# A gated linear attention with an MLP behind it: the odd angles of 64 partitions travel in the carry tile, and the kernel gets another order of work

## The chip, the cores and the metric

The kernel runs on one core of one Trainium2 chip. The metric is the device time of one execution in microseconds (us), the median of three runs. All times below are microseconds unless marked ns. The engines are named as in the profile: PE (matrix products), PEld (loading of their weights), DVE (vector), ACT (scalar and table functions), POOL (general purpose), SP (which only issues DMAs here).

## The reference, cut to what matters

```python
# q, k, v, a_re, a_im: (4 batches, 8 heads, 768 steps, 48)
mag = sqrt(a_re**2 + a_im**2);  scale = minimum(mag, 0.999) / (mag + 1e-6)
ar, ai = a_re * scale, a_im * scale
for t in range(S):                                   # a complex state, 48 x 48 per head
    new_re = ar[t] * S_re - ai[t] * S_im
    new_im = ar[t] * S_im + ai[t] * S_re
    S_re, S_im = new_re + outer(k[t], v[t]), new_im
    y[t] = q[t] @ S_re
x  = y with the heads side by side                   # (4, 768, 384)
xn = (x - mean(x)) / sqrt(var(x) + 1e-6) * g_ln
out = x + maximum(xn @ w_ch1, 0) @ w_ch2             # 384 -> 1536 -> 384
```

The recurrence is computed in chunks of 128 steps. The logarithm of the gate's size and its angle are summed over the steps, which gives decays and phases; q and k are multiplied by them, and what is left is a masked product of q and k, times v, plus the state of the chunk before.

## The kernel before, in words

There are 4 batches of 6 chunks. Two chunks make a **pair**, so there are 12 pairs, P = 0 to 11; chunks are numbered n = 2P and 2P + 1. The first pair of a batch is P = 0, 3, 6, 9. Pair 0 is worked in two halves of four heads (parts), all others in one piece.

For a pair, a partition holds **two neighbouring steps**: partition p has step 2p (j = 0, "even") and 2p + 1 (j = 1, "odd") of the pair's 256. In this layout ACT takes a logarithm (`ln`), an inverse (`iv`), `u` and the arctangent (`th`), and DVE or POOL the products `r` and `r2` and the log-size `l`. Running sums over the steps are products on PE with triangles of ones (`u_e` for sizes, `u_th` for angles in turns), which leave chunk c = 0 and c = 1 in two PSUM banks with one step to a partition. `dec` is the sum of sizes, from which ACT makes the decays `e` and `en`; `ph` is the sum of angles. Chunk 0 needs the odd angles of partitions 0 to 63 alone (the triangle `u_th[:, 0, 1]` is zero below them), chunk 1 needs all.

The **carry**: a phase runs on from pair to pair of a batch. After `ph` of a pair, `car.P` writes rows 96 to 127 of the next pair's tile `car` (fp16, 128 x 384, two in turn) with the last phases; row 64 holds a constant window (`car0`, the tile is filled with it once). `pick` is a weight that is 1 in rows 64 and 127 and 0 elsewhere, so a product with it adds window and carry; `pick_f`, for a batch's first pair, has row 64 alone. A pair's `ph` before is six products of 384 columns: two of angles for each chunk, and one of the carry for each.

From the phases ACT makes sine and cosine (`sin`, `cos`, with `abs` or `qt` between), `ke`, `qe` multiply k and q by the decays, and `ks`, `qs` by sine and cosine. `ksT`, `qsT` are their transposes: on PE through PSUM (`kT`, `qT`, then a copy), or as a DMA transpose that SP issues. `am` is the product of both, `atm` its masking on DVE, `gm` and `G` the state, `y` the output, `x` its copy, `xtr` and `xT` its transpose, `mm1`, `relu` and `mm2` the MLP, `ot` the last sum, and `st` the store. `wp` and `wc` fold the norm into the first weight at the start (weights come by `wl`).

**What sets the order.** One table, `PLAN`, names every step, its engine (P, A, V, G for POOL, S for a DMA issued by SP) and its PSUM bank; each engine runs its steps in this order, and semaphores are placed from what a step reads and writes. `@name` behind a step lets it wait for another on purpose (turns between POOL and DVE). `warm` steps are products of no use (256 columns of `u_e`) that keep PE busy while the first inputs come. A step on the S list waits in line behind those before it; `k`, `q`, `vf`, `are`, `aim` are loads.

```python
for op in steps:
    ...
    op.emit()
```

Of the kernel before, what the change touches and what calls it, by code (L numbers as in the profile page):

```python
# [51 lines left out]
warm.69:P0 warm.70:P0 warm.71:P0 warm.72:P0 warm.73:P0 warm.74:P0 warm.75:P0 dps.0:P5 mask:G are.3.0:S r2.2.0:V
e.1.0:A2 dps.1:P7 ke.0.1.0:V u.2.0:A tab.trig.1:A pad.qs.1:G th.0.1:A vf.0.1:S ke.0.0.0:V th.0.0:A th.1.0:A warm.76:P0
warm.77:P0 warm.78:P0 warm.79:P0 warm.80:P0 warm.81:P0 warm.82:P0 warm.83:P0 warm.84:P0 warm.85:P0 warm.86:P0
warm.87:P0 warm.88:P0 warm.89:P0 warm.90:P0 ph.0.1:P1 qe.0.0.0:V decc.0:V5 qe.0.1.0:V decc.1:V7 l.2.0:V sin.0.1:A1
vf.0.0:S ph.0.0:P3 lc.2.0:V car.0.1:A1 car.0.0:V3 ks.0.1.1:V qs.0.1.1:V warm.91:P0 warm.92:P0 wp.1:P4 wc.1.2:V4
qt.0.1:P1 k.1.1:S wl.0:G th.2.0:A ph.1.0:P6 wc.1.1:V4 wc.1.0:V4 sin.0.0:A3 ke.1.0.0:G@qs.0.1.1 qs.0.0.1:V aim.3.0:S
cos.0.1:A1 qt.0.0:P3 qe.1.0.1:G sin.1.0:A6 cos.0.0:A3 qs.0.1.0:V tab.log.2:A ks.0.0.0:V warm.93:P0 warm.94:P0
warm.95:P0 warm.96:P0 warm.97:P0 warm.98:P0 warm.99:P0 warm.100:P0 warm.101:P0 dec.2.0:P4 ks.0.1.0:V qs.0.0.0:V
q.2.0:S warm.102:P0 warm.103:P0 warm.104:P0 warm.105:P0 warm.106:P0 warm.107:P0 wp.0:P1 en.2.0:A4 ks.0.0.1:V  # L60
qe.1.0.0:G@qs.0.0.0 car.1.0:V6 wc.0.0:V1 kT.0:P2 e.2.0:A4 wc.0.2:V1 qT.0:P3 vf.1.0:S qt.1.0:P6 vf.1.1:S qsT.0:V3
qT.1:P5 ln.3.0:A qs.1.0.1:G warm.108:P0 warm.109:P0 warm.110:P0 warm.111:P0 kT.1:P3 are.4.0:S ksT.0:A2 q.2.1:S
wc.0.1:V1 qsT.1:V5 iv.3.0:A wl.2:G ksT.1:V3 warm.112:P1 am.0:P0 k.2.1:S aim.4.0:S k.2.0:S warm.113:P2 ph.2.0:P4
am.1:P2 tab.trig.3:A atm.0:V0 atm.1:V2 cos.1.0:A6 v.0:G ke.1.0.1:G warm.114:P0 warm.115:P0 gm.0:P7 y.0:P1 sin.2.0:A4
warm.116:P0 warm.117:P0 qt.2.0:P4 G.0:A7 x.0:A1 qs.1.0.0:V gm.1:P7 y.1:P2 cos.2.0:A4 r.3.0:G xtr.0:P6 x.1:A2
ks.1.0.0:V warm.118:P0 qT.3:P1 pad.qs.2:G qT.2:P4 v.1:G th.3.0:A ks.1.0.1:V xT.0:V6 r2.3.0:G@xT.0 xtr.1:P3 kT.3:P0
qsT.3:V1 wp.2:P6 wl.3:G@xT.0 ksT.3:V0 q.3.1:S qsT.2:A4 tab.log.4:A kT.2:P2 qe.2.0.1:G qe.2.0.0:G am.3:P4 xT.1:V3
G.1:V7 mm1.0.0.1:P0 mm1.0.0.0:P0 one:G@ke.0.1.0 ksT.2:A2 gm.2:P7 relu.0.0:A0 wc.2.0:V6 atm.3:V4 wc.2.2:V6 G.2:A7
mm1.0.1.1:P2 ln.4.0:A am.2:P4 mm1.0.1.0:P2 wc.2.1:V6 y.3:P6 relu.0.1:A2 ph.3.0:P0 iv.4.0:A atm.2:V4 x.3:V6 gm.3:P7
y.2:P6 qs.2.0.1:V x.2:A6 xtr.3:P2 mm1.0.2.1:P4 wl.4:G@atm.2 xtr.2:P3 car.3.0:V0 q.3.0:S r.4.0:G are.6.0:S mm1.0.2.0:P4  # L70
bn.1:V xT.3:V2 xT.2:V3 abs.3.0:A0 mm1.1.1.0:P2 u.3.0:A bn.3:V G.3:V7 relu.0.2:V4 mm1.1.1.1:P2 tab.trig.5:A relu.1.1:A2
mm1.1.2.1:P6 sin.3.0:A0 k.3.0:S bn.2:V mm1.1.2.0:P6 k.3.1:S mm1.1.0.0:P3 cos.3.0:A qs.2.0.0:V are.5.0:S mm1.1.0.1:P3
wl.5:G@qs.2.0.1 l.3.0:V th.4.0:A r2.4.0:V lc.3.0:V qT.5:P2 qT.4:P1 ke.2.0.1:G relu.1.2:V6 mm2.0.0:P5 mm2.0.1:P5
relu.1.0:A3 ke.2.0.0:G ks.2.0.0:G@r2.4.0 tab.log.6:A mm2.1.0:P3 u.4.0:A bn.0:V dec.3.0:P6 rstd.0:A mm2.1.1:P3 qsT.4:V1
# [137 lines left out]
def kernel(  # L212
# [12 lines left out]
    nc = tc.nc  # L225
# [617 lines left out]
```

## Time and profile before

| | us |
|---|---|
| three runs | 188.86, 189.84, 190.18; median 189.84 |
| the profiled execution, own time | 189.38 |
| its span on the core | 187.7 |
| busy PE / DVE / ACT / POOL | 175.9 / 159.0 / 156.0 / 95.7 |
| granted PE clock | 1.00 |

A page of the profile has the busy time of each engine, the span in 40 equal slices (digits are tenths busy), the DMA queues, the chain of work that ended last, and the costliest groups of instructions. PE's products are pipelined: the mean of one is its own length from start to end, while a run of them follows at a shorter distance, so the sum of a run is read from a run's length. Between the span and the execution's own time lie 1.68 us.

### The profile page before, as it was taken

Reading aid. Unit: us, or ns where it says so; the run is one execution under the profiler, and the core shown is the slowest. Engines: PE = TensorE matmul, PEld = TensorE weight load, DVE = VectorE, ACT = ScalarE, POOL = GpSimd, SP = SyncE. Lnnn points to the kernel's source line nnn. Section 1 sums busy time; section 2 is a strip of 40 time slices with the busy share of each in tenths; the row PEclk is TensorE's granted clock in tenths of the full one; section 3 lists DMA queues with packets and bytes.
Section 4 is the critical chain, followed back from the end, with each engine's and each line's share of the span. In section 5 each row is a group of like instructions: output and inputs, shape, how many; then the busy total and the mean of one; then the engine's idle time right before and its main releaser. Section 6 shows DMA issues by size and latency. Waiting matters only on the chain.

```text
span 187.7 us, 5141 instructions
## 1 busy us (share of the span) xinstructions
PE 175.9 (94%) x2040; PEld 138.6 (74%) x2040; DVE 159.0 (85%) x292; ACT 156.0 (83%) x223; POOL 95.7 (51%) x117
## 2 busy tenths in 40 slices
PE   5699999999999999999999999999999899797992
PEld 3488677888677897777877877877768577685772
DVE  0599999999989999889999899968999878676463
ACT  5699999999999999999999999988999869143220
POOL 8137387776614990696068570740621507521650
PEclk9999999999999999999999999999999999999999
DMA  5999999999999895899999999999989899996423
GB/s 136 284 243 178 235 237 213 209 191 227 228 235 265 188 263 131 147 219 213 187 244 206 181 245 218 179 227 171 213 188 197 190 210 155 234 121 167 136 98 126
DMA packets 131799, 37.23 MB, mean 198 GB/s; under 512 B 125888, under 2 KB 131776, under 8 KB 131776
## 3 DMA queue, kind: packets, MB, share of 16 engines
q1 hardware_dynamic: 128272, 33.76, 86.5%
q0 software_dynamic: 2784, 2.36, 8.5%
q10 hardware_dynamic: 720, 0.79, 1.2%
q8 instruction: 16, 0.26, 0.5%
q14 instruction: 7, 0.06, 0.1%
HBM read 28.31 MB, written 4.72 MB: 176 GB/s over the span
## 4 chain that ended last, share of the span: by engine, by line
PE 56%; DVE 19%; DMA 13%; issue 3%; SPq 3%; ACT 3%; POOL 1%; DVEq 0%; ACTq 0%; POOLq 0%
PE banks L773 20%; PE banks L741 14%; DMA aim<-in_a_im_dram 5%; DMA qsT<-qs 5%; PE banks L613 5%; PE banks L507 4%; PE banks L636 3%; DVE w1b L392 3%; DVE atm L293 3%; DMA ksT<-ks 2%; PE banks L481 2%; DVE r L293 2%; PE banks L686 2%; PE banks L707 2%; PE banks L689 2%
## 5 line engine op out<-in xcount | busy, mean ns | idle before, releaser
L773 PE MATMUL banks<-w2b,h 128*128 128x384 bf16 (+1 forms) x300 | 54.6, 319 | 0.0
L741 PE MATMUL banks<-xT,w1b 128*128 128x256 bf16 x432 | 51.2, 272 | 0.1
L741 PEld LDWEIGHTS <-w1b 128*128 128x128 bf16 x432 | 41.2, 98 | 6.5 <-DVE xT L290 0.8
L773 PEld LDWEIGHTS <-h 128*128 128x128 bf16 x300 | 26.8, 97 | 12.5
L293 DVE TENSOR_TENSOR atm<-banks,mask 128x1024 bf16<-128x1024 f32 x24 | 28.9, 1219 | 4.8 <-PE banks L636 4.5
L758 ACT ACTIVATE h<-banks 128x1024 bf16<-128x1024 f32 (+1 forms) x25 | 24.9, 1006 | 9.4 <-PE banks L741 9.2
L293 POOL TENSOR_TENSOR ke<-k,en 128x384 bf16<-128x384 f32 x17 | 15.8, 933 | 16.5 <-ACT en L485 4.7
L811 ACT ACT_TABLE_LOAD x18 | 23.1, 1283 | 1.1 <-PEq L827 0.8
L806 PE MATMUL banks<-u_e 128*128 128x256 f16 x119 | 16.7, 289 | 2.5 <-POOL u_e L322 2.2
L636 PE MATMUL banks<-qsT,ksT 128*128 128x128 bf16 x192 | 14.6, 219 | 2.9 <-DMA qsT<-qs 1.8
L760 DVE TENSOR_SCALAR h<-banks 128x1024 bf16<-128x1024 f32 (+1 forms) x12 | 14.0, 1175 | 3.7 <-PE banks L741 3.6
L293 POOL TENSOR_TENSOR qe<-q,e 128x384 bf16<-128x384 f32 x13 | 12.0, 929 | 9.3 <-DVE ks L293 5.3
L636 PEld LDWEIGHTS <-ksT 128*128 128x128 bf16 x192 | 12.2, 98 | 5.0 <-issue 2.3
L806 PEld LDWEIGHTS <-u_e 128*128 128x128 f16 x119 | 12.1, 104 | 4.6 <-POOL u_e L322 1.9
L293 POOL TENSOR_TENSOR r<-aim,are 128x768 f16<-128x768 f32 x6 | 10.9, 1813 | 6.1 <-ACT are L454 5.9
L786 POOL TENSOR_TENSOR ot<-ot,x 128x384 f32<-128x384 f32 x11 | 10.6, 974 | 6.3 <-DVE x L290 4.4
L288 ACT CAST x<-banks 128x384 bf16<-128x384 f32 x16 | 7.7, 483 | 7.2 <-PE banks L689 6.4
L470 DVE SCALAR_TENSOR_TENSOR l<-r,w 128x768 f16<-128x768 f16 (+1 forms) x13 | 12.9, 996 | 0.7 <-ACT r L466 0.6
L699 DVE BATCH_NORM_STATS2 stats<-x 128x6 f32<-128x384 bf16 x24 | 13.2, 550 | 0.3 <-ACT x L288 0.3
L293 POOL TENSOR_TENSOR qs<-qe,trig 128x768 bf16<-128x768 bf16 x6 | 10.3, 1725 | 5.9 <-DVE qe L293 3.5
L418 POOL TENSOR_SCALAR v<-vf 128x768 bf16<-128x768 f32 x8 | 7.0, 869 | 12.0 <-DMA vf<-in_v_dram 7.0
L686 PE MATMUL banks<-v,atm 128*128 128x48 bf16 x192 | 12.1, 183 | 0.2 <-DVE atm L293 0.2
(100 smaller groups left out, 385.0 us busy)
## 6 DMA issues: line engine op xcount, KB each, us to landing
k<-in_k_dram SPq DMA_DIRECT2D x24, 192.0 KB, 4.3
q<-in_q_dram SPq DMA_DIRECT2D x24, 192.0 KB, 4.5
vf<-in_v_dram SPq DMA_DIRECT2D x24, 192.0 KB, 4.1
are<-in_a_re_dram SPq DMA_DIRECT2D x11, 384.0 KB, 4.6
aim<-in_a_im_dram SPq DMA_DIRECT2D x11, 384.0 KB, 4.6
out_dram<-ot SPq DMA_DIRECT2D x20, 192.0 KB, 3.1
w1b<-in_moe_w_ch_dram POOLq DMA_DIRECT2D x3, 384.0 KB, 6.1
w2b<-in_moe_w_ch_dram POOLq DMA_DIRECT2D x3, 384.0 KB, 7.2
```

The costliest lines, as they stand in the source:

```text
L293: {"DVE": nc.vector, "POOL": nc.gpsimd}[eng(name)].tensor_tensor(**kw)
L470: nc.vector.scalar_tensor_tensor(out=S_("l"), in0=S_("r2"), scalar=0.5, in1=S_("w"), op0=ALU.mult, op1=ALU.add)
L636: nc.tensor.matmul(ps[:, h], lhsT=T("ksT", n)[:, h], rhs=T("qsT", n)[:, h], start=True, stop=True)
L686: nc.tensor.matmul(ps[:, h], lhsT=T("atm", n)[:, h], rhs=T("v", P)[:, c, h], start=True, stop=nfirst)
L699: nc.vector.bn_stats(out=T("stats", n), in_=T("x", n))
L741: nc.tensor.matmul(ps[:, jj], lhsT=w1b[:, dc, ts(gi * JG + jj, C)], rhs=T("xT", P)[:, dc].rearrange("p c t -> p (c t)"), start=(dc == 0), ...
L758: act(out=dst, in_=src, func=AF.Relu)
L760: nc.vector.tensor_scalar(out=dst, in0=src, scalar1=0.0, scalar2=None, op0=ALU.max)
L773: nc.tensor.matmul(bank(own)[:, 0:w], lhsT=T("h", P)[:, j, ts(c, C)], rhs=w2b[:, j, es], start=(j == 0), stop=(j == NJ - 1))
L786: nc.gpsimd.tensor_tensor(out=T("ot", n)[:, es], in0=T("ot", n)[:, es], in1=T("x", n)[:, es], op=ALU.add)
L806: g.add(f"warm.{i}", lambda i=i: nc.tensor.matmul(bank(f"warm.{i}")[:, 0:256], lhsT=u_e[:, 0, 0], rhs=u_e[:, 1].rearrange("p j t -> p (j t ...
L811: g.add(f"tab.{nm}.{i}", lambda tab=tab: nc.scalar.preload_act_table_set(tab))
```

## The change

In pairs 1 to 11 the odd angles of partitions 0 to 63 are copied into rows 0 to 63 of the pair's carry tile (a new step, `tc`). Two new weights, `u_car` and `u_car_f`, hold the odd triangle in rows 0 to 63 and `pick` (or `pick_f`) in rows 64 to 127 and are made once by four copies on DVE (`ucar`). Chunk 0 then takes its odd angles and its carry in one product, so that a pair's `ph` is five products. `ph` waits for `tc` and `ucar`. Of the eleven copies eight are on POOL, two on ACT (pairs 10 and 11), one on DVE (pair 9).

The table of work is another one. The `warm` steps are 99 of 256 columns and 23 of 512 (`warmw`) where there were 119 of 256.

```diff
+    u_car = pool.tile([C, C], FP16, name="u_car")
+    u_car_f = pool.tile([C, C], FP16, name="u_car_f")
...
+    def c_ucar():
+        for t, p in ((u_car, pick), (u_car_f, pick_f)):
+            nc.vector.tensor_copy(out=t[HALF:C], in_=p[HALF:C])
+            nc.vector.tensor_copy(out=t[0:HALF], in_=u_th[0:HALF, 0, 1])
...
+            if NS == 1:
+                def f_tc(X=X, fs=fs, step=step):
+                    dst, src = heads(T("car", P)[0:HALF, fs]), step(T("th", P), 1)[0:HALF]
+                    if eng(f"tc.{X}") == "POOL":
+                        nc.gpsimd.tensor_scalar(out=dst, in0=src, scalar1=1.0, scalar2=0.0,
+                                                op0=ALU.mult, op1=ALU.add)
+                    else:
+                        put(f"tc.{X}", dst, src)
+                add(f"tc.{X}", f_tc, needs=[f"th.{X}", f"car0.{P % RINGS['car']}"],
+                    uses=[("th", P), ("car", P)])
...
                     car = T("car", P)[:, fs]
-                    w_car = pick_f if first else pick
                     for c, w, x, start, stop in (
                             (0, u_th[:, 0, 0], th[0], True, False),
-                            (0, u_th[:, 0, 1], th[1], False, False),
                             (1, u_th[:, 1, 0], th[0], True, False),
                             (1, u_th[:, 1, 1], th[1], False, False),
-                            (0, w_car, car, False, True),
-                            (1, w_car, car, False, True)):
+                            (0, u_car_f if first else u_car, car, False, True),
+                            (1, pick_f if first else pick, car, False, True)):
...
-    for i in range(200):
+    for i in range(99):
         g.add(f"warm.{i}", lambda i=i: nc.tensor.matmul(
...
+    for i in range(23):
+        g.add(f"warmw.{i}", lambda i=i: nc.tensor.matmul(
+            bank(f"warmw.{i}"), lhsT=u_e[:, 0, 0], rhs=u_e.rearrange("p c j t -> p (c j t)"),
+            start=True, stop=True), needs=["ue"], ps=(f"warmw.{i}", 1))
```

Counted over the whole table, the steps that change engine, beside `tc`, `ucar` and the fillers, are these (before to after): `ks` on DVE 22 to 16, on POOL 4 to 10; `qs` on POOL 6 to 3; `qe` on POOL 13 to 16; `r` and `r2` on POOL one more each; `v` on ACT 0 to 2, on DVE 4 to 2; `abs` on ACT 7 to 9, on DVE 2 to 0; `xT` on ACT 6 to 8, on DVE 16 to 14; `G` on ACT 9 to 7, on DVE 11 to 13; `rstd` on ACT 6 to 7; the copies of `qsT` on ACT 3 to 2; DMA transposes of `qsT` 11 to 12, so that PE has one `qT` less; six more DMAs are issued by ACT in place of SP (three stores, one `k`, two `vf`).

At three places the new table reads as follows. On SP, the first loads of the program before (`are`, `aim`: the gate's two parts, the number is the buffer; 4x96 is a half of pair 0):

```order
L449 DMA are0_64<-in_a_re_dram 128x4x96 x2
L449 DMA aim0_67<-in_a_im_dram 128x4x96
L449 DMA are1_65<-in_a_re_dram 128x8x96
L449 DMA aim0_67<-in_a_im_dram 128x4x96
L449 DMA aim1_68<-in_a_im_dram 128x8x96
```

and the same place of the change:

```order
L458 DMA are0_64<-in_a_re_dram 128x4x96
L458 DMA aim0_67<-in_a_im_dram 128x4x96
L458 DMA are0_64<-in_a_re_dram 128x4x96
L458 DMA are1_65<-in_a_re_dram 128x8x96
L458 DMA aim0_67<-in_a_im_dram 128x4x96
L458 DMA aim1_68<-in_a_im_dram 128x8x96
```

The first half's `aim` moved from the third place to the second, ahead of the second half's `are`.

On POOL, around the phases of pairs 6 to 8 (in the middle of the program), the steps before are, from `r` of pair 7 to the first product of pair 6:

```order
L293 TENSOR_TENSOR r1_85<-aim1_68,are1_65 128x768 [waits DMAHW5_49,DMAHW2_49,Activation_49]
L293 TENSOR_TENSOR qe1_109<-q2_72,e1_98 128x384 [waits DMAHW3_49,DVE_49,Activation_49]
L293 TENSOR_TENSOR ke1_107<-k2_75,en1_100 128x384 [waits DMAHW6_49,Activation_49]
L293 TENSOR_TENSOR qe1_109<-q2_72,e1_98 128x384 [waits DMAHW4_49]
L293 TENSOR_TENSOR ke1_107<-k2_75,en1_100 128x384 [waits DMAHW7_49,DVE_49]
L293 TENSOR_TENSOR qs2_115<-qe1_109,trig2_103 128x16x48 [waits PE_49,Pool_49]
L293 TENSOR_TENSOR r2_86<-aim2_69,are2_66 128x768 [waits DMAHW3_49,DMAHW2_49,Activation_49]
L293 TENSOR_TENSOR ke0_106<-k0_73,en0_99 128x384 [waits DMAHW6_49,DVE_49]
```

and of the change, from the same `r` on (L505 is the copy `tc`, of pairs 6, 7 and 8 in this order):

```order
L294 TENSOR_TENSOR r1_85<-aim1_68,are1_65 128x768 [waits DMAHW6_49,DMAHW3_49,Activation_49]
L505 TENSOR_SCALAR car0_167<-th0_92 64x384 [waits DVE_49]
L294 TENSOR_TENSOR r2_86<-aim2_69,are2_66 128x768 [waits DMAHW1_49,Activation_49,Pool_49]
L294 TENSOR_TENSOR ke1_107<-k2_75,en1_100 128x384 [waits DMAHW5_49]
L294 TENSOR_TENSOR ke1_107<-k2_75,en1_100 128x384 [waits DMAHW4_49,DVE_49]
L294 TENSOR_TENSOR qe0_108<-q0_70,e0_97 128x384 [waits DMAHW7_49,Activation_49]
L294 TENSOR_TENSOR qe1_109<-q2_72,e1_98 128x384 [waits DMAHW0_49]
L505 TENSOR_SCALAR car1_168<-th1_93 64x384 [waits PE_49,Activation_49]
L505 TENSOR_SCALAR car0_167<-th0_92 64x384 [waits PE_49,DVE_49,Activation_49,Pool_49]
L294 TENSOR_TENSOR ke0_106<-k0_73,en0_99 128x384 [waits DMAHW2_49]
```

Each copy stands behind an `r` or behind several `ke` and `qe` of POOL's queue; PE's `ph` of pairs 6, 7 and 8 waits for these three copies.

On SP, near the end, the transposes of chunks 18 and 19 (pair 9; buffers 2 and 3 of `ksT` and `qsT`) stand before in one block behind a `k` load:

```order
L408 DMA k1_74<-in_k_dram 128x8x48 [waits DMAHW0_49]
L618 DMA_TRANSPOSE qsT2_122<-qs0_113 128x8x128 [waits DMAHW1_49,DVE_49,PE_49]
L618 DMA_TRANSPOSE ksT2_118<-ks0_110 128x8x128 [waits DMAHW2_49,DVE_49]
L618 DMA_TRANSPOSE ksT3_119<-ks0_110 128x8x128 [waits DMAHW3_49]
L618 DMA_TRANSPOSE qsT3_123<-qs0_113 128x8x128 [waits DMAHW4_49,Activation_49]
L408 DMA q1_71<-in_q_dram 128x8x48 [waits DMAHW5_49]
```

and in the change:

```order
L417 DMA k1_74<-in_k_dram 128x8x48 [waits DMAHW0_49]
L637 DMA_TRANSPOSE qsT3_123<-qs0_113 128x8x128 [waits DMAHW1_49,DVE_49,PE_49]
L417 DMA vf1_77<-in_v_dram 128x8x48 [waits DMAHW2_49,Activation_49]
L637 DMA_TRANSPOSE qsT2_122<-qs0_113 128x8x128 [waits DMAHW4_49,PE_49]
L417 DMA vf1_77<-in_v_dram 128x8x48 [waits DMAHW5_49]
L637 DMA_TRANSPOSE ksT2_118<-ks0_110 128x8x128 [waits DMAHW6_49,DVE_49,Pool_49]
L637 DMA_TRANSPOSE ksT3_119<-ks0_110 128x8x128 [waits DMAHW7_49]
```

Both `qsT` now go ahead of both `ksT`, with the loads of `v` between them.

More of the change, by code (lines that the diff above doesn't have):

```diff
@@ L60 @@
[L60 to L74, printed above, removed]
```

194 lines of the change are left out of this document (106 added, 88 removed).

## The prediction

> **What bounds the kernel now.** I read the busy times and the slices first, then windows by stage, then the chain that ended last, then the single waits of PE.
>
> ```profile
> PE 175.9 (94%) x2040; PEld 138.6 (74%) x2040; DVE 159.0 (85%) x292; ACT 156.0 (83%) x223; POOL 95.7 (51%) x117
> ...
> PE   5699999999999999999999999999999899797992
> ...
> DVE  0599999999989999889999899968999878676463
> ACT  5699999999999999999999999988999869143220
> ```
>
> A slice is 4.7 us. PE is full from the third slice to the 31st (12 to 143 us), and ACT and DVE are nearly as full up to the 31st. The windows say it more finely; the columns are PE, PEld, DVE, ACT and POOL busy, with the number of instructions:
>
> ```profile
> 60.00:70.00 10.00, 10.00 (x167) 8.64 (x164) 9.79 (x16) 9.71 (x14) 10.00 (x10) 1.00 1.01 229
> 110.00:120.00 10.00, 10.00 (x115) 7.82 (x113) 9.41 (x16) 9.47 (x15) 4.54 (x6) 1.00 0.98 220
> ```
>
> Up to about 120 us PE, ACT and DVE are all saturated, so less work on PE pays only as far as ACT and DVE keep up. Behind it ACT and DVE have air, and PE waits, each time for a transpose that SP sends through the DMA engines (in brackets the idle time and what ended it):
>
> ```profile
> 148.75 0.61 PE L636 MATMUL banks<-qsT,ksT 128*128 128x128 bf16 x8 [0.84 <-DMA qsT<-qs]
> 160.58 0.62 PE L636 MATMUL banks<-qsT,ksT 128*128 128x128 bf16 x8 [1.12 <-DMA ksT<-ks]
> 170.35 0.61 PE L636 MATMUL banks<-qsT,ksT 128*128 128x128 bf16 x8 [0.62 <-DMA qsT<-qs]
> 171.65 0.61 PE L636 MATMUL banks<-qsT,ksT 128*128 128x128 bf16 x8 [0.33 <-DMA qsT<-qs]
> ```
>
> These are chunks 19, 20, 22 and 23, together 2.91.
>
> **The products.** The chain has PE's runs with their true length:
>
> ```profile
> 58.18 0.98 PE banks L507 x6
> 55.94 0.47 PE banks L613 x8
> ```
>
> Six products of a phase take 0.98, one 0.163. Eleven pairs lose one: 11 x 0.163 = -1.79. The new order also sends one more `qsT` through the DMA engines, which takes eight transposes from PE: -0.47. Both lie where PE is full, so by PE alone they count whole.
>
> **The start.** PE has fillers there, and their number changed.
>
> ```profile
> 2.22 4.25 PE L806 MATMUL banks<-u_e 128*128 128x256 f16 x24 [2.22 <-POOL u_e L322]
> 8.33 0.49 PE L481 MATMUL banks<-l,u_e 128*128 128x192 f16 x4 [1.86 <-DVE l L473]
> 13.64 2.13 PE L806 MATMUL banks<-u_e 128*128 128x256 f16 x18
> 19.47 0.81 PE L388 MATMUL banks<-w1b,gc 128*128 128x512 bf16 x3
> 32.22 0.27 PE L806 MATMUL banks<-u_e 128*128 128x256 f16 x1
> ```
>
> A run of 18 fillers has 2.13 from first start to last end, and its last one's own length is near 0.27; (2.13 - 0.27) / 17 = 0.109 each. The first 24 take 0.17 each, a start-up cost of some 1.6 that both orders have. For a filler of 512 columns the nearest row is the weight product of 512: (0.81 - 0.38) / 2 = 0.215, taking its last one's own length at 0.38, its share of 1.4 times the 0.27 of a filler. So the fillers go from 119 x 0.109 = 13.0 to 99 x 0.109 + 23 x 0.215 = 15.7, +2.8. That is no cost by itself: between 2.22 and the last filler's end at 32.5 PE has 30.3, of which fillers are 13.0, the start-up 1.6 and useful products about 11.4 (counted from the table with the chain's run lengths); 4.3 is gaps. If the new fillers lie in these gaps, the place is reached up to 4.3 - 2.8 = 1.5 sooner; the one gap that they fill for certain is the 1.86 ahead of the first sum, so at worst it comes 2.8 - 1.9 = 0.9 later.
>
> What sets the gaps is the first `r`, on DVE:
>
> ```profile
> 5.88 0.56 DVE L293 TENSOR_TENSOR r<-aim,are 128x384 f16<-128x384 f32 x1 [4.64 <-DMA aim<-in_a_im_dram]
> 7.42 0.56 DVE L470 SCALAR_TENSOR_TENSOR l<-r,w 128x384 f16<-128x384 f16 x1 [0.59 <-ACT r L466]
> ...
> 1.85 0.50 SPq L449 DMA_DIRECT2D aim<-in_a_im_dram  x1
> ```
>
> SP issues its `aim` third, at 1.85, for 0.50, and now second, so half a microsecond sooner; `r` can start as much sooner. The second half's `are` goes back by as much, and ACT takes it before `u`; I take half a microsecond of gain at the start, -0.5, with the ends -1.5 and +0.9. The four copies of `ucar` stand between `r2` and `l` on DVE, where DVE idles 0.59; four small copies at some 0.16 (the `pick_f` write of 1x128 has 165 ns) are 0.6: I cost them at nothing, at +0.6 if the idle time is gone.
>
> **ACT.** By the counts of the table ACT gets two `v` (as `th`, 0.85), two `tc` and two `xT` (as `G`, 0.48), two `abs` (0.81) and an `rstd`, and loses a `qsT` (1.04), two `G` and the first `car0`, which with the `rstd` I set against each other:
>
> ```profile
> L489 ACT ACTIVATE th<-r 128x768 f16<-128x768 f16 x11 | 9.3, 850 | 0.1
> L550 ACT ACTIVATE sh<-banks 128x768 f16<-128x768 int16 x7 | 5.7, 812 | 0.0
> L288 ACT CAST G<-banks 128x384 bf16<-128x384 f32 x9 | 4.3, 477 | 1.7 <-PE banks L664 1.7
> L288 ACT COPY qsT<-banks 128x1024 bf16<-128x1024 bf16 x3 | 3.1, 1039 | 0.0
> ```
>
> 1.7 + 1.0 + 1.0 + 1.6 - 1.0 - 1.0 = +3.3, less than half of it before 120 us. Six more DMAs stand in its queue. The one place where a DMA stands between two of ACT's steps is in the tail:
>
> ```profile
> 180.51 0.60 ACT L758 ACTIVATE h<-banks 128x512 bf16<-128x512 f32 x1 [5.74 <-PE banks L741]
> 180.59 0.34 ACTq L796 DMA_DIRECT2D out_dram<-ot  x1
> 181.04 0.58 ACT L779 ACTIVATE ot<-banks,rstd 128x384 f32<-128x384 f32 x1
> ```
>
> Its 0.34 lies inside the 0.60 before it, so nothing; at most 0.34 each. I take +0.7 for ACT, with the ends 0 and +2.3 (all that PE gains by products and transposes is then hidden).
>
> **POOL and DVE.** DVE is relieved of six `ks`, three `qe`, two `abs`, two `xT`, two `v`, an `r` and an `r2`, and gets three `qs`, two `G` and the new copies; at its half a microsecond for most of them that is some 6 less. POOL gets eight copies, six `ks`, three `qe`, an `r` and an `r2`, and loses three `qs` and an `rstd`.
>
> ```profile
> L293 POOL TENSOR_TENSOR ke<-k,en 128x384 bf16<-128x384 f32 x17 | 15.8, 933 | 16.5 <-ACT en L485 4.7 <-DVE ke L293 4.5 <-ACT car L525 2.9
> L293 POOL TENSOR_TENSOR r<-aim,are 128x768 f16<-128x768 f32 x6 | 10.9, 1813 | 6.1 <-ACT are L454 5.9
> L293 POOL TENSOR_TENSOR ks<-ke,trig 128x768 bf16<-128x768 bf16 x4 | 6.7, 1687 | 7.0 <-DVE ke L293 3.4 <-DVE r L293 2.3 <-DVE mv L700 1.2
> L418 POOL TENSOR_SCALAR v<-vf 128x768 bf16<-128x768 f32 x8 | 7.0, 869 | 12.0 <-DMA vf<-in_v_dram 7.0 <-DVE ot L789 2.6 <-DVE qsT L290 2.3
> ```
>
> A copy of 64 x 384 was never run there. The nearest row is `v`, the same kind of instruction at 768 columns: half of it is 0.43, its whole 0.87 the other end. With the rows for the rest POOL's work grows by about 13 us, from 95.7 to 109, still 58% of the span. It is not full, but its queue is in order: PE's `ph` waits for the copy, the copy stands behind what is ahead of it, and behind it wait the `ke` that feed `ks`. For pair 7 an `r`, two `ke` and two `qe` (1.81 + 4 x 0.93 = 5.5) stand between the copies of pairs 6 and 7. And the two engines get in each other's way:
>
> ```profile
> L293 DVE TENSOR_TENSOR ks<-ke,trig 128x768 bf16<-128x768 bf16 x18 | 9.7, 553 | 0.5 <-POOL ke L293 0.4
> ...
> 91.35 0.95 DVE L470 SCALAR_TENSOR_TENSOR l<-r,w 128x768 f16<-128x768 f16 x1
> 101.46 1.14 DVE L470 SCALAR_TENSOR_TENSOR l<-r,w 128x768 f16<-128x768 f16 x1
> 101.75 1.63 POOL L786 TENSOR_TENSOR ot<-ot,x 128x384 f32<-128x384 f32 x1
> 111.34 0.91 POOL L786 TENSOR_TENSOR ot<-ot,x 128x384 f32<-128x384 f32 x1
> 111.56 1.51 DVE L470 SCALAR_TENSOR_TENSOR l<-r,w 128x768 f16<-128x768 f16 x1
> ```
>
> At 101.46 DVE began first, and POOL's 0.91 became 1.63, ending at 103.4; at 111.34 POOL began first, and DVE's `l`, 0.95 at 91.35, took 1.51. So a meeting costs the later one 0.6 to 0.7. I take +0.8 for all of it: of 14 more POOL steps, one in ten or so meets something on the path. The ends are 0 and what the rival below gives. [...]
>
> **The late waits.** The new order puts both `qsT` of pair 9 ahead of its `ksT`, on SP, so that only two transposes are left when the last `ks` is done. For pair 10, PE now has the state product, two outputs, three parts of `mm2`, two small transposes, a phase and four parts of `mm1` between `am` of chunks 19 and 21, about 6.9; DVE needs a mask (1.2) and a `ks` (0.55), and a transpose some 5 from its issue, as the chain has it:
>
> ```profile
> L293 DVE TENSOR_TENSOR atm<-banks,mask 128x1024 bf16<-128x1024 f32 x24 | 28.9, 1219 | 4.8 <-PE banks L636 4.5
> ...
> 143.64 4.97 DMA qsT<-qs
> ```
>
> 1.75 + 4.97 = 6.7 is just below 6.9, where PE waited 1.12 before. I take -1.2 of the 2.91; the ends are -2.5 and 0.
>
> **The sum**, against the profiled execution's 189.38 (span 187.7 and 1.68 around it): -1.79 - 0.47 - 0.5 + 0.7 + 0.8 - 1.2 = -2.46, which gives 186.9. That execution lies 0.46 below the median of 189.84; I forecast **187.0**, a gain of 1.5% on the median. The bound is 1% of it, 1.9 us, about what a measurement of this kernel can tell from no change: below 187.9 is faster, above 191.7 slower.
>
> **The rivals.**
>
> *ACT stays the bound.* For: 9.5 to 9.9 of every 10 us up to 120, and it gets more work. PE's 2.3 then turns into waits for `e`, `relu` and `x`, and only start and late waits remain, with 0.8 for POOL and 0.5 for ACT work that nothing absorbs: 189.38 - 0.5 - 1.2 + 0.8 + 0.5 = 189.0. Against: PE is as full, and DVE's relief can bring ACT's inputs sooner. Chance 0.31.
>
> *POOL's queue holds the phases: slower.* If POOL loses 0.7 to a meeting, as at 101.75, ahead of each of its eight copies, and the copies had no lead, PE waits about 0.8 at each `ph`: 8 x 0.8 = 6.4 in place of my 0.8. 189.38 - 3.26 + 6.4 = 192.5. It decides from 0.7 a copy on (then 191.7). For: POOL at 10.00 of 10 in 60 to 70 and more now, 5.5 of queue ahead of a copy. Against: `th` is ready long before its `ph` in most pairs, and PE has other work listed ahead. [...] Chance 0.17.
>
> *All falls well.* Late waits gone (-2.5), start -0.9, ACT and POOL at nothing: 189.38 - 2.26 - 0.9 - 2.5 = 183.7. Chance 0.06.
>
> The forecast keeps 0.46. Faster is 0.52, same 0.31, slower 0.17. The range goes from 184.5, which leaves out the best case, to 192.0, which leaves out the upper part of the slow one.
>
> **What would show it.** `ph` in groups of five, with no idle time ahead that a POOL copy ended: products right. The first `r` near 5.4 and the second pair's first transposes near 32: start right. PE's waits on DMA transposes under 2 in all: late waits right. PE idle between 40 and 120 ended by ACT: the first rival; ended by POOL, or DVE `l` and `ks` well above 1.1 and 0.55: the second. I am wrong if a load or a weight comes too late on the reordered SP and POOL queues, which no term here holds.

## The result, and the profile after

The kernel after takes **191.27 us** (median of 20 runs, 190.22 to 193.06), before 189.39 beside it (20 runs, 188.21 to 190.89): a ratio of **1.0103, 95% interval [1.0073, 1.0134]**. It is slower by 1%, where 187.0 was forecast. Measured twice more, on two chips, it had 1.0197 [1.0139, 1.0255] and 1.0127 [1.0071, 1.0183]. The ratios here leave out runs that lie over 1.5% above the fastest of their kernel; some kernels below scatter by more, and for those the medians of all runs are given.

The page of the changed kernel, for the lines shown of before (its profiled execution has 192.58, 1.3 above the median):

```profile
PE 178.4 (94%) x2022; PEld 137.7 (72%) x2024; DVE 155.1 (81%) x285; ACT 158.8 (83%) x230; POOL 108.0 (57%) x131
...
PE   5994988999999999999999999999999799998992
...
DVE  2797298799989999987999799999889577496662
ACT  4799199899999999999999999999999868554210
...
PEclk9998899999999999999999999999999999999999
```

The busy times are near what was counted (POOL 109 forecast, 108.0 here; ACT +3.3 counted, +2.8 here). What is new stands at the left: a 4 in the fourth slice of PE (14 to 19 us; a slice is 4.8), a 1 and a 2 in the fifth of ACT and DVE, and a granted clock of 8 in both. The timeline of PE in that place, first of before, then of after:

```profile
16.17 1.80 PE L806 MATMUL banks<-u_e 128*128 128x256 f16 x15
17.81 0.25 PE L511 MATMUL banks<-car,pick 96*128 96x192 f16 x1
...
32.32 1.06 PE L613 MATMUL banks<-ident,qs 128*128 128x128 bf16 x16
```

```profile
7.91 0.49 PE L490 MATMUL banks<-l,u_e 128*128 128x192 f16 x4
...
15.15 0.54 PE L611 MATMUL banks<-ident,e 128*128 128x1 bf16 x16 [0.30 <-POOL ident masks.py:199]
17.87 4.34 PE L825 MATMUL banks<-u_e 128*128 128x256 f16 x26 [2.18 <-DVE dec L291]
22.05 0.25 PE L529 MATMUL banks<-car,pick 96*128 96x192 f16 x1
...
29.15 1.03 PE L825 MATMUL banks<-u_e 128*128 128x256 f16 x8 [1.41 <-DVE w1b L401]
...
38.14 1.06 PE L632 MATMUL banks<-ident,qs 128*128 128x128 bf16 x16
```

Row 22.05 is the first phase, `ph.0.1`; 38.14 are the transposes of the second pair that the prediction named as its mark. **The first sum of sizes comes sooner (7.91, before 8.33), the mark 5.82 later.** Between them stand 26 fillers that waited 2.18 us for DVE, and 8 that waited 1.41. A filler needs no input that is late: it waits for the bank that it writes to. The table has these steps in this order (`V0` and `P0` mean bank 0):

```
dps.1:P0 qe.0.0.0:V decc.1:V0 l.2.0:V th.0.1:A vf.0.0:S dps.0:P2 th.0.0:A warm.35:P0 ... warm.60:P0 ph.0.1:P3
```

`decc.1` is the copy of `dps.1` out of bank 0 (line L291, tile `dec`). In the same trace it is late on DVE, and the two engines that wait for the first phase stand still:

```profile
17.50 0.32 DVE L291 COPY dec<-banks 48x8 f32<-48x8 f32 x2
23.33 0.36 DVE L547 TENSOR_SCALAR car<-banks 32x192 f16<-32x192 int16 x1 [3.47 <-PE banks L533]
```

```profile
17.36 1.67 ACT L498 ACTIVATE th<-r 128x384 f16<-128x384 f16 x3
22.75 0.49 ACT L552 ACTIVATE trig<-banks 128x384 bf16<-128x384 int16 x1 [3.73 <-PE banks L533]
```

The first of the three `th` was there by 18, so from then on only the fillers held the phase. And in this execution the pause costs twice, as windows of half a microsecond show (columns as before, the granted clock is the third number from the end):

```profile
17.00:17.50 0.50, 0.00 (x0) 0.00 (x0) 0.50 (x3) 0.49 (x2) 0.00 (x0) 0.74 1.21 185
17.50:18.00 0.50, 0.13 (x1) 0.10 (x1) 0.46 (x4) 0.50 (x2) 0.00 (x0) 0.50 1.19 195
...
20.50:21.00 0.50, 0.50 (x6) 0.40 (x5) 0.00 (x0) 0.00 (x0) 0.00 (x0) 0.85 1.20 188
```

The windows from 15.00 to 17.00 have 1.00 and those from 17.50 to 20.50 have 0.50, so a mean of 0.74 is full clock for 0.48 of that window and half after it: the clock falls to 0.50 at 17.24; by the 0.85 it returns at 20.65. The 26 fillers take 4.34 for that reason. Not every execution pays this: of the 20, five have a mean granted clock of 0.991, as this one, and a median of 192.60; the other 15 have 0.998 or more and 190.90, and are still slower than before. At full clock a run of 26 takes 3.00 (a row below). The first phase is late by 2.18 of waiting, 1.34 of half clock and 11 more fillers than before at 0.109, 1.2; less the half microsecond by which the start was sooner, that is 4.2, and 22.05 - 17.81 is 4.24.

From the mark to the end after has 190.8 - 38.14 = 152.7, before 187.7 - 32.32 = 155.4: **2.7 us won back behind the start**, not enough for the 5.8 lost in it. In two more profiles of after, the second with the clock at 1.00 throughout, 5.3 and 4.2 are lost and 2.0 and 1.7 won.

### The profile page after: what moved, and what is told of

Its sections match the earlier page's. It is cut to its first block, busy times and chain, and to the rows that moved or that the text cites. A ratio compares the mean times of both kernels' runs of the same rounds, so it can differ in the third digit from the quotient of the medians.

```text
span 190.8 us, 5133 instructions
## 1 busy us (share of the span) xinstructions
PE 178.4 (94%) x2022; PEld 137.7 (72%) x2024; DVE 155.1 (81%) x285; ACT 158.8 (83%) x230; POOL 108.0 (57%) x131
## 3 DMA queue, kind: packets, MB, share of 16 engines
q10 hardware_dynamic: 4272, 1.97, 3.6%
## 4 chain that ended last, share of the span: by engine, by line
PE 64%; DMA 10%; DVE 8%; ACT 7%; SPq 4%; issue 4%; POOL 1%; DVEq 0%; POOLq 0%
PE banks L792 21%; PE banks L760 15%; PE banks L655 5%; PE banks L632 4%; PE banks L825 4%; PE banks L525 4%; DMA qsT<-qs 4%; PE banks L490 3%; DMA aim<-in_a_im_dram 3%; DMA q<-in_q_dram 3%; PE banks L705 2%; SPq L637 2%; PE banks L726 2%; PE banks L708 2%; DMA vf<-in_v_dram 2%
## 5 line engine op out<-in xcount | busy, mean ns | idle before, releaser
L294 POOL TENSOR_TENSOR ks<-ke,trig 128x768 bf16<-128x768 bf16 x10 | 16.3, 1638 | 12.6 <-DVE ke L294 8.8
L294 POOL TENSOR_TENSOR qe<-q,e 128x384 bf16<-128x384 f32 x16 | 14.5, 913 | 8.3 <-ACT e L494 4.8
L825 PE MATMUL banks<-u_e 128*128 128x256 f16 x99 | 14.1, 291 | 3.6 <-DVE dec L291 2.2
L294 POOL TENSOR_TENSOR r<-aim,are 128x768 f16<-128x768 f32 x7 | 12.7, 1808 | 4.5 <-DVE mv L719 4.5
L825 PEld LDWEIGHTS <-u_e 128*128 128x128 f16 x99 | 10.2, 104 | 6.2 <-issue 3.9
L552 ACT ACTIVATE trig<-banks 128x768 bf16<-128x768 int16 (+1 forms) x13 | 9.9, 762 | 4.8 <-PE banks L533 3.7
L294 DVE TENSOR_TENSOR qs<-qe,trig 128x768 bf16<-128x768 bf16 (+1 forms) x23 | 12.9, 583 | 0.0
L461 ACT ACTIVATE w<-are 128x768 f32<-128x768 f32 (+1 forms) x13 | 10.4, 799 | 2.6 <-DMA are<-in_a_re_dram 2.6
L479 DVE SCALAR_TENSOR_TENSOR l<-r,w 128x768 f16<-128x768 f16 (+1 forms) x13 | 11.6, 892 | 1.0 <-ACT r L475 0.8
```

Of the source, the lines that this page charges most:

```text
L294: {"DVE": nc.vector, "POOL": nc.gpsimd}[eng(name)].tensor_tensor(**kw)
L461: add(f"ln.{X}", lambda S_=S_: act(out=S_("w"), in_=S_("are"), func=AF.Ln), needs=[f"are.{X}"], uses=[("are", P), ("w", P)])
L479: nc.vector.scalar_tensor_tensor(out=S_("l"), in0=S_("r2"), scalar=0.5, in1=S_("w"), op0=ALU.mult, op1=ALU.add)
L825: g.add(f"warm.{i}", lambda i=i: nc.tensor.matmul(bank(f"warm.{i}")[:, 0:256], lhsT=u_e[:, 0, 0], rhs=u_e[:, 1].rearrange("p j t -> p (j t ...
```

## The experiments

The expectations call PE TensorE, DVE VectorE, ACT ScalarE and POOL GpSimd. In the first four the theory is that the start is lost to the fillers' banks; rival 1 is that the fillers are too many, rival 2 that the new order of loads, of DVE and of ACT is late. In the later ones the rival is that ACT's full row takes the gain of the products.

### The banks of the fillers

```diff
-warm.35:P0 ... warm.60:P0
+warm.35:P1 ... warm.60:P1
```

> The changed kernel with one thing other: the 26 fillers ahead of the first phase go to PSUM bank 1, which is free, in place of bank 0, which the copies of dec still hold. Theory (the fillers wait for the bank): PE starts them at about 15.7 in place of 17.87, has them done by 18.6 at full clock, the first phase moves from 22.05 to 18.3 to 18.8, and the time falls from 191.3 by 3 to 4, to 187.3 to 188.3. Rival 1 (too many fillers, wherever they are, and the slow clock comes from the wide ones): the phase stays at 20 or later, gain under 1.5. Rival 2 (the start is late because of the new order of loads, of DVE and of ACT): no gain beyond 0.5.

Measured: 189.18 us (188.62 to 191.82, 10 runs), 1.0021 [0.9989, 1.0052] of before. In its profile the 26 start at 15.75 without a wait, and the first phase at 18.58, as the theory has it; of the 3 to 4 us that it gives, 1.6 came by the ratios (1.0103 to 1.0021). The same with the second group moved as well:

```diff
-warm.70:P1 ... warm.77:P1
+warm.70:P0 ... warm.77:P0
```

> As the kernel with 26 fillers in bank 1, and the eight fillers ahead of the first transposes also moved, from bank 1, which a weight fold of DVE holds until 29.1, to bank 0. Theory: the wait of 1.41 at 29.15 goes too; time 0.8 to 1.4 below the kernel with one group moved, 186.0 to 187.3. Rival 2: same as the changed kernel within 0.5. A second rival for this step alone: the transposes then wait for qs, so the gain is under 0.4.

Measured: 188.74 us (187.73 to 190.88, 10 runs), 0.9994 [0.9962, 1.0027]. This is called "the mended kernel" below. PE's timeline in it:

```profile
15.27 3.00 PE L825 MATMUL banks<-u_e 128*128 128x256 f16 x26
18.11 0.25 PE L529 MATMUL banks<-car,pick 96*128 96x192 f16 x1
...
33.28 1.06 PE L632 MATMUL banks<-ident,qs 128*128 128x128 bf16 x16
```

The same 26 fillers run without a wait at full clock, and the mark is 4.86 sooner than in the profile of after above (3.2 sooner than in the one at full clock). The expectation was met in its direction and missed in its size: 2.1 us reach the end by the ratios (1.0103 to 0.9994, each against before beside it).

The rival, fillers too many, is tried by leaving the 26 out:

```diff
-warm.35:P0 ... warm.60:P0
```

> The changed kernel without these 26 fillers, all else kept; no result changes. Theory: the first phase starts when the arctangent is there, at 18.0 to 18.4; time 187.3 to 188.5, at the upper end if the PE clock falls in the idle stretch of 2.3 us. Rival 1: as good as or better than moving the bank, since fewer fillers are what counts. Rival 2: no gain beyond 0.5.

Measured: 191.49 us (190.06 to 193.50, 4 runs), 1.0125 [1.0071, 1.0179], no faster than after. PE's timeline, and its windows:

```profile
17.80 0.48 PE L530 MATMUL banks<-th,u_th 128*128 128x192 f16 x2 [2.58 <-ACT th L495]
```

```profile
17.00:17.50 0.50, 0.00 (x0) 0.00 (x0) 0.50 (x1) 0.49 (x2) 0.00 (x0) 0.57 1.10 174
...
23.50:24.00 0.50, 0.50 (x3) 0.26 (x2) 0.50 (x2) 0.50 (x2) 0.00 (x0) 0.61 0.75 159
```

The products of the first phase run from 17.80, as early as before, but PE idles 2.58 ahead of them, and the clock is at 0.50 from 17.07 to 23.9: now the useful products run at half speed (a carry and its two angle products take 0.48 us here, from 18.08 to 18.56, and 0.25 in the mended kernel, from 18.11 to 18.36). All four executions have a mean granted clock of 0.980 to 0.991; the 20 of the two kernels with moved fillers, on the same chip, have 0.996 or more. The mark is at 35.26, sooner than in after, and the time is no better. So rival 1 fails: with the 26 in a free bank the kernel is at 1.0021, without them at 1.0125.

And the reverse: the bank's wait put into the kernel before, whose 15 fillers ahead of the same phase go behind `decc.1` and into its bank.

```diff
-warm.76:P0 ... warm.90:P0 ph.0.1:P1 qe.0.0.0:V decc.0:V5 qe.0.1.0:V decc.1:V7
+qe.0.0.0:V decc.0:V5 qe.0.1.0:V decc.1:V7 warm.76:P7 ... warm.90:P7 ph.0.1:P1
```

> The kernel before with one thing other: the 15 fillers ahead of its first phase go to bank 7, which the second copy of dec holds until about 18.2, in place of bank 0. Theory: PE idles from 16 to 18.2 and then runs 15 fillers, the first phase moves from 17.8 to 20 or 20.5, and the time rises from 189.4 by 1.7 to 2.8, to 191.1 to 192.2. Rival 1: the number of fillers is the same, so no change beyond 0.5. Rival 2: no change beyond 0.5.

Measured: 191.35 us (190.25 to 192.62, 4 runs), 1.0145 [1.0080, 1.0211]. PE's timeline shows the same wait, and the mark 1.54 later than before:

```profile
18.32 1.80 PE L800 MATMUL banks<-u_e 128*128 128x256 f16 x15 [1.97 <-DVE dec L284]
...
33.86 1.06 PE L607 MATMUL banks<-ident,qs 128*128 128x128 bf16 x16
```

Putting the wait in costs the kernel before 2.7 us by the ratio (four runs); taking the same one out of after gives 1.6. The cause of the lost start is shown from both sides. It isn't the whole of it: with both banks mended the mark is at 33.28, 32.93 and 34.45 in three profiles, still 0.6 to 2.1 later than before.

### Where the rest of the gain goes

The mended kernel is level with before here, not 2 us faster. In the middle ACT, and PE behind it, meet a wait in it that after had not; the second of PE's two rows, for `v`, is in after too (1.20):

```profile
80.07 0.84 ACT L461 ACTIVATE w<-are 128x768 f32<-128x768 f32 x1 [1.07 <-DMA are<-in_a_re_dram]
```

```profile
81.67 0.81 PE L490 MATMUL banks<-l,u_e 128*128 128x384 f16 x4 [0.94 <-ACT en L494]
...
146.69 0.36 PE L683 MATMUL banks<-v,ks 128*128 128x48 bf16 x8 [0.88 <-POOL v L427]
```

The first row belongs to the logarithm of pair 8. Without the wait it would start at 79.0, 4.6 sooner than after has it (83.55). SP issues its load at 75.05 in place of 76.29, only 1.2 sooner, as the two timelines of SP have it, after first (in both SP sends one DMA right behind the other there):

```profile
76.29 1.42 SPq L458 DMA_DIRECT2D are<-in_a_re_dram  x1
```

```profile
75.05 1.52 SPq L458 DMA_DIRECT2D are<-in_a_re_dram  x1
```

The loads did not come forward with the work. Three small mends were tried on the mended kernel, and one run leaves stores out.

```diff
-warm.78:P1 ... warm.89:P1
-warm.90:P2 ... warm.96:P2
```

> The same kernel with mended banks, without the 12 fillers ahead of the first scores am.0 and the 7 ahead of ph.2.0 (19 x 0.11 = 2.05 us on TensorE). If the fillers still hold the start up, the second transposes come 0.5 to 1.0 us sooner than 33.28 and the time falls by as much: 187.7 to 188.3, ratio 0.994 to 0.997. If ScalarE, busy without a gap from 20 to 35 us, sets the start by then, no change (ratio 0.998 to 1.001). If the clock falls in the gaps that they leave, slower, 1.003 or more, with a granted clock under 0.9 between 25 and 35 us.

Measured: 191.48 us (189.21 to 194.30, 12 runs), 1.0071 [1.0032, 1.0109]; the mark at 32.75, 0.53 sooner as expected, but inside the spread of the mended kernel's own marks (32.93 to 34.45). The loads of `v` of pair 9, sooner on SP:

```diff
-q.10.0:S ... qsT.19:S ... vf.9.1:S ... qsT.18:S ... vf.9.0:S
+vf.9.1:S vf.9.0:S q.10.0:S ... qsT.19:S ... qsT.18:S
```

> The same kernel with mended banks, with the two loads of v of pair 9 (vf.9) issued on SP ahead of the loads q.10.0 and the transposes xT.16, qsT.19, qsT.18, in place of between them. TensorE waited 0.9 us for v.9 at 146. If that wait lies on the path, 0.5 to 0.9 us faster: ratio 0.994 to 0.997. If the transposes that now stand behind the loads are late instead, or ScalarE is, no change: 0.998 to 1.002.

Measured: 191.40 us (189.44 to 195.05, 12 runs), 1.0076 [1.0036, 1.0117]; PE's wait for `v` is gone, and it waits 1.0 for `xT` and 1.1 for `ksT` instead. These two ran on another chip than the mended kernel, which was therefore measured there too, with after beside it:

> The kernel with both groups of fillers in free banks, again, on the chip of this call: its two close variants (no fillers 78 to 96; loads of v of pair 9 earlier) were at 1.007 to 1.008 of before elsewhere, where it had 0.999 itself. If the mended banks are worth 2.5 us, as first measured, this is at 0.985 to 0.990 of the kernel after beside it, and at 0.997 to 1.001 of before. If the gain was a matter of the chip, it stands within 0.5% of the kernel after.

Measured: 192.59 us (190.38 to 195.56, 6 runs), 1.0119 [1.0045, 1.0193].

> The kernel after, unchanged, beside the next three on one chip, so that they can be set against it directly. Expected as first measured: ratio to before 1.007 to 1.013.

Measured: 193.19 us (191.80 to 193.73, 6 runs), 1.0197 [1.0139, 1.0255]. So on this chip the banks are worth 0.6 us by the medians and 0.8% by the ratios, whose intervals overlap: a gain can't be told from noise here, and neither of the two guesses of the expectation is decided. Nor can the two small mends be told from the mended kernel (191.5 and 191.4 against 192.6). Without the stores of the first four chunks:

```diff
-ring(f"st.{n}{tag}").dma_start(
+n > 3 and ring(f"st.{n}{tag}").dma_start(
```

> The kernel with mended banks, which leaves out the stores of the first four output chunks (st.0 to st.3, 4 x 192 KB of the 37.5 MB; these rows of the output are not written). The DMA engines are busy in nearly every slice, and ScalarE waited 1.07 us for are.8 at 80 us. If the DMA stream paces the middle, are.8 comes 2 us or more sooner, that wait is gone and the time falls by 1 us or more: ratio to the kernel with mended banks 0.990 to 0.995. If ScalarE's own row paces it, no change: 0.997 to 1.003.

Measured: 191.95 us (189.37 to 194.67, 12 runs), 1.0078 [1.0029, 1.0127]. The wait for `are` is gone, and ACT's tenth load of a function table, a mark of how far it is, comes at 84.8 (85.9, 86.2 and 86.3 in three profiles of the mended kernel), its 14th at 127.4 (128.4, 128.8, 129.1), its last at 153.3 (153.3, 153.8, 155.2). In its one profile the middle is 1.0 to 1.7 us sooner without these stores; against two of the three profiles 0.0 and 0.5 of the lead are left at 153, and by the times no gain can be told from noise. The third mend, and all of them together, on a further chip with the mended kernel for a measure:

```diff
-aim.8.0:S y.5:P4 ... l.6.0:V are.8.0:S
+are.8.0:S y.5:P4 ... l.6.0:V aim.8.0:S
```

> The kernel with mended banks, with the loads are.8 and aim.8 exchanged in SP's order (so that are.8 is issued some 15 us sooner, where aim.8 stood). In the two profiles of the kernel with mended banks ScalarE stood for are.8 at 80 us and TensorE behind it for 0.9 and 1.7 us. If that load is what the mended start runs into, both waits are gone and the time falls by 0.9 to 1.7 us against the same kernel in this call (ratio to it 0.991 to 0.996). If the time is given back later, as where the stores were left out, no change (0.997 to 1.003).

Measured: 191.66 us in the median of all 12 runs (189.11 to 193.92); 1.0020 [0.9970, 1.0069] by the ratio. In its profile SP issues `are` of pair 8 at 67.24, and ACT's wait for it is gone. The mended kernel beside it (the run after next) has 192.10: 0.4 us more by the medians of all runs, 1.0% by the ratios. A gain is likely, its size is open.

> The kernel with mended banks and all three small mends together: are.8 for aim.8, the loads of v of pair 9 ahead of the transposes, and no fillers 78 to 96. If each takes a wait off the path, 0.9 to 1.7 + 0.5 to 0.9 + 0.5 less: 1.9 to 3.1 us under the kernel with mended banks, ratio to before 0.990 to 1.000 on a chip where that has 1.01. If ScalarE's row or the DMA stream takes it all back, within 0.4% of it.

Measured: 190.87 us in the median of all 12 (187.68 to 192.62); 0.9966 [0.9914, 1.0018].

> The kernel with mended banks once more, as the measure for the other three on this chip. So far 0.999 and 1.012 of before; if it depends on the chip, it falls to one of the two, with the length of ScalarE's wait for are.8 to tell them apart (1.1 us where it was at 0.999).

Measured: 192.10 us (191.65 to 193.49, 6 runs), 1.0122 [1.0073, 1.0172]. The three mends together seemed to be worth 1.2 us, so they were measured once more beside after:

> The kernel with all four mends (both groups of fillers in free banks, are.8 for aim.8, the loads of v of pair 9 earlier, no fillers 78 to 96), once more, beside the kernel after on the same chip, to see whether it beats both. From the first time (190.9 where before had 190.0, half of its runs between 187.7 and 190.9): within 0.7% of before, ratio 0.994 to 1.004, and 1.0 to 2.0% below the kernel after. If the mends had only luck on that chip, it is within 0.5% of the kernel after.

Measured: 191.96 us in the median of all 12 (189.31 to 195.32), 1.0053 [1.0011, 1.0096].

> The kernel after, unchanged, beside the one with all mends: 1.010 to 1.020 of before, as in the two calls so far.

Measured: 192.01 us (190.76 to 193.84, 6 runs), 1.0127 [1.0071, 1.0183]. The medians are the same, and the ratios 0.7% apart with intervals that overlap: **no version was found that beats both kernels.**

Set against the median of before beside it, run by run, the kernels stand so (all runs on all chips together; s.d. is that of one run):

| | runs | median | s.d. |
|---|---|---|---|
| after | 32 | 1.0124 | 0.005 |
| banks mended | 22 | 1.0072 | 0.010 |
| banks and the three others | 24 | 1.0061 | 0.010 |
| the last two, each with six products | 12 | 1.0123 | 0.005 |

and by their profiles:

| profiled execution | mark (us) | mark to end | span |
|---|---|---|---|
| before | 32.32 | 155.4 | 187.7 |
| after, three | 38.14, 37.63, 36.48 | 152.7, 153.4, 153.7 | 190.8, 191.0, 190.2 |
| banks mended, three | 33.28, 32.93, 34.45 | 153.7, 155.8, 155.4 | 187.0, 188.7, 189.9 |
| all mends, the shorter of two | 32.73 | 153.3 | 186.0 |
| six products, banks mended | 33.42 | 157.9 | 191.3 |
| six products, all mends | 33.95 | 156.6 | 190.6 |

With the banks mended the mark is 3.9 us earlier in the mean, and what follows 1.7 longer. In the same profiles PE's waits behind 40 us are 2.0, 2.7 and 2.7 in after, and 2.5, 4.5 and 4.0 in the mended kernel, most of it for `qsT` (0.7, 1.8 and 1.9) and the decays. That accounts for 1.2 of the 1.7. Which transfer it is differs from run to run, and where `v` was mended the wait moved to the next. What the rest is, is not shown.

### What five products are worth

The mended kernel with the six products of before, without `tc` and `ucar`:

```diff
-(0, u_car_f if first else u_car, car, False, True),
+(0, u_th[:, 0, 1], th[1], False, False),
+(0, pick_f if first else pick, car, False, True),
```

> The kernel after with both groups of fillers in free banks (188.7 us, 0.999 of before), but with six products again for a pair's phases and without the copies tc and ucar. If the products are worth their time on TensorE, as the prediction has it (11 x 0.163 = 1.79 us), this is 1.8 us slower: 190.5, ratio to before about 1.009. If ScalarE sets the pace where these products stand (9.9 of 10 busy from 50 to 150 us), TensorE's saved time only becomes idle time there and this is within 0.5 us of 188.7, ratio 0.997 to 1.003; the time between the first and the last carry product would be the same in both.

Measured: 192.07 us (190.39 to 193.15, 6 runs), 1.0125 [1.0074, 1.0177]; the two five-product variants beside it had 191.48 and 191.40. The same with all mends:

> The same with all mends, with six products again and neither tc nor ucar: what the products are worth where no load or bank holds the rows. Products worth their time: 1.8 us slower than the kernel with five beside it (ratio to it 1.009). ScalarE's row the bound: within 0.4%.

Measured: 192.50 us (190.81 to 193.42, 6 runs), 1.0119 [1.0063, 1.0175], beside 190.87 with five. So the products are worth 0.6 and 1.6 us in two pairs of measurements. The kernel that differs from the first by nothing but the products, with their copies, is the mended one; on the same chip it had 192.59, which would leave them nothing. Over all runs of the table the kernels with five stand at 1.0072 and 1.0061 and those with six at 1.0123, about 1.0 us, with some 0.5 of standard error by the s.d. of the table. (From the mark on, 156.6 and 153.3 in the second pair's profiles would give 3.3, but 153.3 comes from the fastest of that kernel's 12 runs.) So neither the rival, that ACT takes their whole gain, nor the full 1.79 is shown.

The five products alone, in the order of before, each copy right behind its `th` in the queue of POOL (pairs 1 to 8; one line of eleven):

```diff
-th.4.0:A
+th.4.0:A tc.4.0:G
```

> The kernel before, in its own order and with its own fillers, with the five products alone: ucar behind uth on VectorE, each tc behind its th (pairs 1 to 8 on GpSimd, 9 on VectorE, 10 and 11 on ScalarE). By the prediction's sum 1.79 us less plus up to 0.8 for the copies: 187.4 to 188.4 where before has 189.2, ratio 0.990 to 0.995. If ScalarE sets the pace, 0.998 to 1.003. If GpSimd's queue holds the phases (the prediction's slower rival), above 1.005, with TensorE idle ahead of the carry products.

Measured: 200.20 us (198.34 to 202.92, 6 runs), **1.0528 [1.0472, 1.0584]**. The view of the copy's line:

```profile
L499 POOL TENSOR_SCALAR car<-th x8: 501/504/513, 20.0 to 96.1; 64x384 f16<-64x384 f16 x8
...
its engine sat idle before it (us, times) until:
  ACT th L492: 8.5, 6
```

The longest of these waits on POOL's timeline, and what PE waits for 6 us later:

```profile
49.54 0.51 POOL L499 TENSOR_SCALAR car<-th 64x384 f16<-64x384 f16 x1 [4.14 <-ACT th L492]
```

```profile
55.89 0.62 PE L626 MATMUL banks<-ident,ks 128*128 128x128 bf16 x8 [1.60 <-POOL ks L288]
```

POOL stood 8.5 us for `th` with `ke` and `ks` behind it in line, and at this place PE paid 1.60 for it: it waited for the `ks` behind the copy, not at the phase, as the slower rival has it. The standing is no price by itself: the mended kernel's POOL stands 8.9 us ahead of five such copies and is level with before on the first chip. Which of the later waits go back to it is not shown. With the copies of pairs 1 to 9 on DVE instead:

> The kernel before with the five products alone, as in the run where GpSimd copied, but the nine copies of pairs 1 to 9 are made by VectorE (0.25 us each by the one such row of the kernel after), two or three steps behind the th in its queue; pairs 10 and 11 on ScalarE. If it was GpSimd's queue, standing at the copy until th was there, that cost 10 us, they are gone: 0.992 to 1.003 of before. By the prediction's sum, -1.79 on TensorE and up to +0.5 for copies in full rows, 0.993. If instead the five products or the copy itself cost the time, it stays above 1.03.

Measured: 195.86 us (194.97 to 197.88, 6 runs), 1.0356 [1.0296, 1.0415]. Taking the copies off POOL gave back 4.3 us by the medians; the rest stays, and is not one wait: ACT's table loads fall behind those of before by 1.5 at the third, 2.4 at the fifth, 3.2 at the eighth and 5.7 at the ninth. Beside such a loss the products can't be priced in the old order.

## Why the prediction was wrong, by its own steps

**The start** is the step that failed: -0.5, with the ends -1.5 and +0.9, where it is +5.8 (5.3 and 4.2 in the two other profiles of after). "If the new fillers lie in these gaps" was asked of their number and their time, and not of their banks: 34 of them stand behind a read by DVE of the bank that they write. The clause "at worst it comes 2.8 - 1.9 = 0.9 later" took fillers for work that only adds its own length. It left out the wait of an engine's whole queue (2.18 and 1.41 us of PE in the profile of after), and what the clock does in it (0.50 for 3.4 us there). The first half of the step was right: `r` began at 4.84 (5.4 forecast), since `aim` came sooner. With the banks mended the start is still +0.6 to +2.1; what holds that part is not shown.

```profile
4.84 0.56 DVE L294 TENSOR_TENSOR r<-aim,are 128x384 f16<-128x384 f32 x1 [1.60 <-DMA aim<-in_a_im_dram]
```

**The rest of the sum**, -1.79 - 0.47 + 0.7 + 0.8 - 1.2 = -1.96, came out at -2.7, -2.0 and -1.7 in the three profiles of after, so the sum held for a kernel that starts late; its terms were not measured one by one, and part of the agreement may be chance. In the execution with 192.58 the start is 6.3 worse than forecast and the rest 0.7 better, which is 5.6 of the 5.7 between it and the 186.9 of the sum. The rest did not add to an early start (-1.7, +0.4 and +0.1 with the banks mended): the sum took its terms as independent, and an early start met loads and transposes that did not come as much sooner. By PE's waits above that is 1.2 of the 1.7 us that are missing.

**The products.** Groups of five, and no wait that a copy on POOL ended, from 40 us on:

```profile
88.68 0.65 PE L525 MATMUL banks<-th,u_th 128*128 128x384 f16 x3
89.17 0.33 PE L525 MATMUL banks<-car,u_car_f 128*128 128x384 f16 x1
89.33 0.33 PE L525 MATMUL banks<-car,pick_f 128*128 128x384 f16 x1
```

**The late waits** went from 2.91 to 0.81 (1.3 and 1.2 in the two other profiles), better than the -1.2 that was taken, but a wait of 1.20 for `v` of pair 9 is new (1.42 and 1.54), as the last sentence of the prediction feared of loads on the reordered queue:

```profile
138.19 0.61 PE L655 MATMUL banks<-qsT,ksT 128*128 128x128 bf16 x8 [0.26 <-DMA qsT<-qs]
150.71 0.36 PE L683 MATMUL banks<-v,ks 128*128 128x48 bf16 x8 [1.20 <-POOL v L427]
172.49 0.61 PE L655 MATMUL banks<-qsT,ksT 128*128 128x128 bf16 x8 [0.55 <-DMA qsT<-qs]
```

**The copy on POOL** takes 0.50 (the longest 0.53) where 0.43 was taken, and three of the eight stand for `th`:

```profile
L505 POOL TENSOR_SCALAR car<-th x8: 501/504/530, 19.1 to 94.9; 64x384 f16<-64x384 f16 x8
...
its engine sat idle before it (us, times) until:
  ACT th L498: 6.1, 3
```

**The rivals.** "POOL's queue holds the phases" gave 192.5, near the measured time, by a mechanism that the trace does not have: POOL does stand at the copies, but no product of PE waits for a copy, and the one wait of PE behind 40 us that POOL ends is that for `v`. The other sign is absent too: DVE's `l` takes 0.95 in the mean and its `ks` 0.55. That the value is near is luck. "ACT stays the bound" has the right neighbourhood, 189.0, for the mended kernel on the first chip; but its sign, PE idle between 40 and 120 until ACT is done, is absent in after and is 0.2 to 1.7 us in the mended kernel, behind ACT's wait for a load.

**Still open** is why the mended kernel was level with before on the first chip and 1% behind it on two others. This difference is much of its s.d. of 1.0% in the table: within one chip it is 0.5%, 1.1% and 0.4%, where after has 0.5%, 0.4% and 0.6%. The waits that grow are those for DMA transposes and loads, and no single one of them was shown to decide.

## What to carry to other kernels

A filler is not free work: it takes a PSUM bank, and if that bank is still to be read, the filler holds its whole engine until the read is done (PE stood for 2.18 and 1.41 us in after, and for 1.97 in the kernel before with its fillers in the other bank), so look up who reads a bank last before giving it to work of no use. Where PE must wait for an input, filler in a free bank can be worth its place for the clock: with the 26 in a free bank the mean granted clock was 0.996 or more and the time 1.0021 of before, without them 0.980 to 0.991 and 1.0125. And a gain at the start need not reach the end, where loads behind it don't follow (here the mark came 3.9 us sooner in the mean, and what follows took 1.7 longer); measure it at the end, not at a mark.

## What the runs showed of the hardware

The granted clock fell to 0.50 in pauses of PE of 2.18 and 2.58 us, above, and of 1.60 in the second profile of after. It did not fall in a pause of 1.97 in the kernel before with its fillers behind the copy, nor in one of 1.05 in the third profile of after. The rows are the second profile of after, then a window of the kernel before with the bank's wait, in the middle of its pause:

```profile
17.14 4.56 PE L825 MATMUL banks<-u_e 128*128 128x256 f16 x26 [1.60 <-DVE dec L291]
```

```profile
17.50:18.00 0.50, 0.00 (x0) 0.00 (x0) 0.50 (x2) 0.49 (x2) 0.49 (x1) 1.00 1.20 213
```

So it isn't the length of the pause alone, and after had the low clock (0.991 in the mean) in 5 of its 20 executions only. The low stretches lasted 3.4 us in after (17.24 to 20.65) and 6.8 without the 26 fillers (17.07 to 23.9, its end by the mean of 0.61). Sixteen products of one column (0.54 us) stand ahead of the pause of 1.60; they stand ahead of that of 1.97 too, so they don't tell the two apart. What decides whether the clock falls is not shown.
